# New costs, resources and ranks for the attention scheduler of a fused attention and mixture-of-experts kernel on one core

## The chip, the cores and the metric

The kernel runs on one core of a Trainium2 chip. The metric is the device time of one execution in microseconds, taken before the change from three runs; one more execution was profiled. TensorE is called PE here, VectorE DVE, ScalarE ACT, GpSimd POOL and SyncE SP.

## The reference

Three stages follow each other: windowed attention, a top-1 mixture of experts with a capacity, and a dense two-layer block with softplus. All is float32.

```python
# q, k, v: (2, 8, 768, 64); 8 global keys, a window of 96
scores = scale * q @ k.T + bias            # bias = -slope[h] * distance
scores = where(is_global | is_local, scores, -1e9)
a = softmax(scores);  x = (a @ v) -> (1536, 512)
# experts: E = 8, D = 512, F = 1024, capacity 384
e = argmax(x @ w_gate);  gate = max of softmax(x @ w_gate)
y = gate * (relu(x @ w1[e]) @ w2[e])       # rows over capacity give 0
# dense block: 512 -> 2048 -> 512
out = softplus(y @ w_in) @ w_out
```

## The kernel before, in words

The tokens are 12 tiles of 128 (2 batches of 6). Tiles 0 and 6 start a batch and have scores of 128 columns (short tiles); the others have 232, the window and the globals before it and the tile's own keys. The attention stage is followed by the expert stage (8 experts, their weights streamed from HBM) and the dense block; each of these begins when its input is there, and in the expert stage a step issues the loads of later weights itself.

For each tile i attention has these steps, which the code calls jobs. LD and LV load q, k and v by SP's queue (`load`, `load_v`). PQ and PK transpose q and k on PE (`prep`), Q and K copy them from PSUM (`keep`). S are the eight score matmuls (`scores`). B adds the bias and takes the maximum on DVE, one per head (`biased`); M1 writes one head's row of the long-tile bias table; E is the exponential on ACT with its sum (`expo`, sums in `den`). T transposes the probabilities of two heads on PE and C copies them (`transp`); V is P times V in two halves (`pv`); OT copies the result (`keep_o`). L, CH, G, R, SL choose the expert and the row's slot (`logits`, `choose`, `gate`, `ranks`, `slots`); X, N, SC transpose the rows back, weight them and scatter them to `xs_d` on POOL. DUP and VP copy the window's part of k and v for the next tile on POOL. ZF writes a block of zeros to `xs_d` (18 of them, by SP), CL and CV load and convert a piece of the dense block's weights (`conv_load`, `conv_step`; CV has one ACT and three DVE instructions), PU starts the load of expert 0's weights. At the end XR, FB and FA build the first expert's input on PE (`first_base`, `first_add`), and ST and CNT count.

The program of each engine is a fixed list, executed in order, each instruction waiting by semaphores for what it needs. This order is made when the kernel is built, by `arrange`: it takes again and again the job that can start first by its own times, and among equals the one of lowest rank (tile number plus `RANK`). A job has a cost per engine on which it may run, jobs it must follow, buffers it takes and gives back (`sizes`), a lag, and an earliest time `at`. Copies from PSUM may run on ACT or DVE; `LEAN` is a handicap for DVE there. The costs are used for the order alone; the chip knows nothing of them.

```python
key = (max(s, free[e] + SLACK) + (LEAN if e == "DVE" and len(x.cost) > 1 else 0.0), x.rank, s + c)
```

PSUM has eight banks: A (2) for preps, one part of the scores, logits, ranks and rows; B (3) for the other scores; C (2) for T; D (1) for P times V. In SBUF there are 8 score buffers `s_sb` (NS), 6 for transposed probabilities (NPT), 2 for q and k as loaded, 3 for v.

Of the kernel before, what the change touches and what calls it, by code (L numbers as in the profile page):

```python
# [96 lines left out]
class Job:  # L97

    def __init__(self, name, cost, run, after=(), take=(), give=(), rank=0.0, lag=0.1, at=0.0):
        self.name, self.cost, self.run, self.after, self.take, self.give = name, cost, run, after, take, give  # L100
        self.rank, self.lag, self.at = rank, lag, at


def arrange(jobs, sizes, free):
# [4 lines left out]
    while left:  # L109
# [33 lines left out]
SLACK, LEAN = 0, 0  # L143
RANK = {
# [223 lines left out]
def fast_path(ctx, tc, q, k, v, n_global, n_local, w_gate, w1, w2, cap, w_in, w_out, out, const):  # L368
# [87 lines left out]
    NS, NPT, NOT = 8, 6, 2  # L456
# [355 lines left out]
    def expo(n):  # L812
# [3 lines left out]
        if i not in dens:  # L816
            dens[i] = a2.tile([P, H], F32, name="den", bufs=3)
# [47 lines left out]
    def choose(i):  # L865
# [10 lines left out]
        ohb = a2.tile([P, E], BF16, name="ohb")  # L876
# [201 lines left out]
    either = lambda c: {"ACT": c, "DVE": c}  # L1078
    n_t = len(tiles)
    job(("TRI",), {"DVE": 0.5}, lambda e: start_tri(), [("M1", 0)])  # L1080
    for j in range(NSLOT // P):
        job(("ZF", j), {"SP": 0.1}, lambda e: zero_fill(1), at=10.0 + 1.9 * j)
    for i, (b, t) in enumerate(tiles):
        N, half = n_t - 1, 0.5 if t == 0 else 1.0
        prev = lambda *names: [(x, i - 2) for x in names] if i >= 2 else []
# [381 lines left out]
```

## Time and profile before

| what | value |
|---|---|
| median of 3 runs | 588.85 us (587.49 to 588.96) |
| the profiled execution | 588.03 us, span 586.1 us |
| mean granted clock of PE | 0.985 |
| PE busy | 557.9 us, 95% |
| DVE busy | 341.8 us, 58% |
| ACT busy | 275.9 us, 47% |
| POOL busy | 89.3 us, 15% |
| DMA | 91.86 MB, mean 157 GB/s |

The span is the time from the first to the last instruction; the rest of the profiled execution's time lies around it. The page's busy shares are means over stages with different limits, so the stages have to be read apart, by the table by stretches and by the timelines. A busy PE in the profile is not a PE at its peak, since ends of matmuls are modelled; start to start of neighbouring instructions is the safer measure.

### The profile page before, as it was taken

The page shows a single profiled execution, that of the slowest core. Times are in us where ns is not written, and L with a number is a line of the kernel's source. Part 1 is how long each engine was busy: PE and PEld are TensorE (multiplying, and loading weights), DVE is VectorE, ACT ScalarE, POOL GpSimd, SP SyncE. Part 2 cuts the span into 40 slices and gives each one's busy share as a digit, 9 for nine tenths or more (in the row PEclk, how much of TensorE's full clock was granted, in tenths as well). Part 3 has the DMA queues.
Part 4 walks back from the last instruction along what each step waited for, and adds up shares of the span by engine and source line. Part 5 has one row for each costly group of instructions (what it writes and reads, how often), then busy time and mean ns, then how long its engine had stood idle before and what let it go on. Part 6 is the DMA issues. An engine that isn't in the chain of part 4 may idle for free. (4 is left out here: it accounts for less than half of the span.)

```text
span 586.1 us, 9980 instructions
## 1 busy us (share of the span) xinstructions
PE 557.9 (95%) x3446; PEld 489.1 (83%) x3446; DVE 341.8 (58%) x998; ACT 275.9 (47%) x682; POOL 89.3 (15%) x123
## 2 busy tenths in 40 slices
PE   4889878989999999999999999999999999999995
PEld 3778756878999999999999888888888888888874
DVE  6677856874777873231575775654785363333451
ACT  3676946842664752322544454444554334323330
POOL 4101322110000000000354142100240020200201
PEclk9799979999999999999999999999999999999999
DMA  7996567825688779998844574432421200100101
GB/s 143 238 267 182 160 157 209 285 89 181 217 283 276 244 237 388 379 310 291 305 154 96 117 108 93 91 118 81 127 81 47 91 1 0 55 18 1 72 21 58
DMA packets 90832, 91.86 MB, mean 157 GB/s; under 512 B 43205, under 2 KB 61661, under 8 KB 90773
## 3 DMA queue, kind: packets, MB, share of 16 engines
q1 hardware_dynamic: 82709, 74.35, 43.7%
q10 hardware_dynamic: 5760, 10.49, 5.6%
q0 software_dynamic: 2304, 6.30, 2.9%
q8 instruction: 29, 0.48, 0.3%
q14 instruction: 30, 0.25, 0.1%
HBM read 71.71 MB, written 19.41 MB: 155 GB/s over the span
## 5 line engine op out<-in xcount | busy, mean ns | idle before, releaser
L1342 DVE SCALAR_TENSOR_TENSOR sa<-ps_m,sa 128x512 f32<-128x512 f32 x48 | 33.2, 692 | 106.9 <-ACT sa L1341 106.9
L1339 ACT ACTIVATE sa<-ps_m 128x512 f32<-128x512 f32 x48 | 28.7, 598 | 136.5 <-PE ps_m L1232 136.5
L1230 PE MATMUL ps_m<-zh,w1s 128*128 128x512 f32 x192 | 75.2, 392 | 0.0
L1231 PE MATMUL ps_m<-zl,w1s 128*128 128x512 f32 x192 | 74.8, 390 | 0.0
L1230 PE MATMUL ps_o<-w2s,g 128*128 128x512 f32 x192 | 74.8, 390 | 0.0
L1232 PE MATMUL ps_o<-w2s,g 128*128 128x512 f32 x192 | 74.8, 390 | 0.0
L1232 PE MATMUL ps_m<-zh,w1s 128*128 128x512 f32 x192 | 74.8, 389 | 0.0
L1231 PE MATMUL ps_o<-w2s,g 128*128 128x512 f32 x192 | 74.7, 389 | 0.0
L493 POOL TENSOR_TENSOR w1s<-raw,w1s 128x512 fp32r<-128x512 f32 x16 | 23.2, 1468 | 241.7 <-ACT w1s L505 241.6
L1281 PE MATMUL ps_y<-h,w 128*128 128x232 f32 (+4 forms) x320 | 59.1, 328 | 0.0
L1254 PE MATMUL ps_h<-xT,w 128*128 128x232 f32 (+4 forms) x320 | 58.7, 327 | 0.0
L819 ACT ACTIVATE s_sb<-s_sb,negm 128x232 f32<-128x232 f32 (+1 forms) x96 | 44.7, 468 | 25.4 <-DVE xg L923 19.2
L1254 PEld LDWEIGHTS ps_h<-xT,w 128*128 128x128 f32 x320 | 52.9, 190 | 0.7 <-ACT xT L1209 0.2
L1281 PEld LDWEIGHTS ps_y<-h,w 128*128 128x128 f32 x320 | 52.3, 190 | 0.5
L1230 PEld LDWEIGHTS ps_m<-zh,w1s 128*128 128x128 f32 x192 | 36.1, 188 | 8.3 <-DVE sa L1342 0.9
L1232 PEld LDWEIGHTS ps_o<-w2s,g 128*128 128x128 f32 x192 | 36.0, 188 | 7.9 <-DVE g L1350 0.4
L1230 PEld LDWEIGHTS ps_o<-w2s,g 128*128 128x128 f32 x192 | 36.0, 188 | 7.6 <-DVE g L1349 0.3
L1232 PEld LDWEIGHTS ps_m<-zh,w1s 128*128 128x128 f32 x192 | 36.0, 188 | 7.6
L1231 PEld LDWEIGHTS ps_o<-w2s,g 128*128 128x128 f32 x192 | 36.1, 188 | 7.5
L1231 PEld LDWEIGHTS ps_m<-zl,w1s 128*128 128x128 f32 x192 | 36.0, 188 | 7.5 <-DVE zl L1289 0.2
L1263 ACT ACTIVATE h<-ps_h 128x232 f32<-128x232 f32 (+4 forms) x40 | 13.3, 332 | 59.9 <-PE ps_h L1254 57.3
L86 DVE SCALAR_TENSOR_TENSOR ct<-csq,ct 128x256 int32<-128x256 int32 x64 | 33.2, 519 | 12.2 <-ACT csq L82 11.8
(208 smaller groups left out, 1133.6 us busy)
## 6 DMA issues: line engine op xcount, KB each, us to landing
w<-in_moe_w_dram SPq DMA_DIRECT2D x20, 1024.0 KB, 7.7
raw<-in_moe_w_dram SPq DMA_DIRECT2D x24, 512.0 KB, 5.3
cr<-in_moe_w_in_dram ACTq DMA_DIRECT2D x20, 256.0 KB, 3.3
cr<-in_moe_w_out_dram ACTq DMA_DIRECT2D x20, 256.0 KB, 3.9
xs_d<-early SPq DMA_DIRECT2D x18, 256.0 KB, 4.0
wi_d<-ct SPq DMA_DIRECT2D x32, 128.0 KB, 5.0
wo_d<-ct SPq DMA_DIRECT2D x32, 128.0 KB, 5.1
raw<-wi_d SPq DMA_DIRECT2D x8, 512.0 KB, 5.3
```

Of the source, the lines that this page charges most:

```text
L86: nc.vector.scalar_tensor_tensor(t, in0=u.bitcast(I32), scalar=3, in1=t, op0=ALU.logical_shift_left, op1=ALU.bitwise_or)
L493: eng.tensor_tensor(lo, raw, f32(hi), op=ALU.subtract)
L819: nc.scalar.activation(s_sb, s_sb, AF.Exp, bias=negm[:, n:n + 1], scale=-1.0, accum_out=dens[i][:, h:h + 1])
L1230: nc.tensor.matmul(ps, hi_l, hi_r, start=first, stop=False)
L1231: nc.tensor.matmul(ps, hi_l, lo_r, start=False, stop=False)
L1232: nc.tensor.matmul(ps, lo_l, hi_r, start=False, stop=last)
L1254: nc.tensor.matmul(ps, w[:, c, js], x[:, c, :], start=c == 0, stop=c == NC - 1)
L1263: nc.scalar.activation(h[:, :n], ps, AF.Relu)
L1281: nc.tensor.matmul(ys[ui, d], w[:, j, sl], h, start=f == 0, stop=f == NFE - 1)
L1339: nc.scalar.activation(a, ps, AF.Abs)
L1342: nc.vector.scalar_tensor_tensor(a, in0=ps, scalar=0.0, in1=a, op0=ALU.max, op1=ALU.add)
```

## The change

The change gives the scheduler other numbers and two new things. DMA transfers get costs as if SP's queue were an engine that moves the data (LD 2.9, LV 1.5, ZF 0.75, PU 5.0 instead of 0.1 to 0.3, with shorter lags), the zero fills may start from 21 us on instead of 10, and a job can also occupy a second engine (`also`: CV now takes 0.7 of ACT). Costs of single jobs are set anew, with copies at 0.47 (ACT) and 0.61 (DVE) of a unit instead of equal, LEAN is 0.3 instead of 0, and all 35 ranks are new. Ten score buffers instead of 8, eight for transposed probabilities instead of 6, six for `den` instead of 3, three for the one-hot rows instead of 2. The work itself is the same, instruction for instruction; order and engines change. All lines behind the first hunks move down by two or three, so L797 (scores) becomes L799, L737 and L739 (copies on ACT and DVE) become L739 and L741, and L1254 (the first expert matmul) L1257.

```diff
-    def __init__(self, name, cost, run, after=(), take=(), give=(), rank=0.0, lag=0.1, at=0.0):
+    def __init__(self, name, cost, run, after=(), take=(), give=(), rank=0.0, lag=0.1, at=0.0, also=()):
...
         free[e] = s + x.cost[e]
+        for o, c in x.also:
+            free[o] = max(free[o], s) + c
...
-SLACK, LEAN = 0, 0
+SLACK, LEAN = 0, 0.3
 RANK = {
-    "B": -2.6, "C": -1.84, "CH": 10.69, "CL": 12.72, "CNT": 9.95, "CV": -15.21, "DUP": 13.9, "E": -0.74, "FA":
+    "B": -12.52, "C": 9.58, "CH": -2.65, "CL": 10.16, "CNT": 7.36, "CV": 25.77, "DUP": 29.55, "E": 44.85,
...
-    NS, NPT, NOT = 8, 6, 2
+    NS, NPT, NOT = 10, 8, 2
...
-            dens[i] = a2.tile([P, H], F32, name="den", bufs=3)
+            dens[i] = a2.tile([P, H], F32, name="den", bufs=6)
...
-        ohb = a2.tile([P, E], BF16, name="ohb")
+        ohb = a2.tile([P, E], BF16, name="ohb", bufs=3)
...
-    either = lambda c: {"ACT": c, "DVE": c}
+    either = lambda c: {"ACT": 0.47 * c, "DVE": 0.61 * c}
...
-        job(("ZF", j), {"SP": 0.1}, lambda e: zero_fill(1), at=10.0 + 1.9 * j)
+        job(("ZF", j), {"SP": 0.75}, lambda e: zero_fill(1), at=21.0 + 1.7 * j)
...
-            job(("LD", i), {"SP": 0.2}, lambda e, i=i: load(i), prev("PQ", "PK") if i > 2 else [], lag=5.0)
+            job(("LD", i), {"SP": 2.9}, lambda e, i=i: load(i), prev("PQ", "PK") if i > 2 else [], lag=2.0)
...
-            job(("E", i, m), {"ACT": 0.5 if t else 0.42}, lambda e, n=n: expo(n), [("B", i, m)])
+            job(("E", i, m), {"ACT": 0.475 if t else 0.395}, lambda e, n=n: expo(n), [("B", i, m)])
...
-            job(("CV", i), {"DVE": 1.05}, lambda e: conv_step(1), [("B", i, H - 1)])
+            job(("CV", i), {"DVE": 1.02}, lambda e: conv_step(1), [("B", i, H - 1)], also=[("ACT", 0.7)])
...
-            job(("PU", i), {"SP": 0.3}, lambda e: pump(-1, 0), [("S", i)])
+            job(("PU", i), {"SP": 5.0}, lambda e: pump(-1, 0), [("S", i)])
```

What this does to the order is seen at three places. The first is PE's list from the scores of tile 0 (`qT_156`) to those of tile 1 (`qT_157`) and behind them. Before:

```order
L797 MATMUL ps_s<-kwin_130,qT_156 128x128 x8
L748 MATMUL ps_prep<-ident,kr 128x128 x4
L830 MATMUL ps_pt<-ident,s_sb 128x128 x2
L748 MATMUL ps_prep<-ident,qr 128x128 x4
L748 MATMUL ps_prep<-ident,kr 128x128 x4
L748 MATMUL ps_prep<-ident,qr 128x128 x4
L830 MATMUL ps_pt<-ident,s_sb 128x128 x2
L849 MATMUL ps_pv<-pT,vt_125 64x128 x4
L797 MATMUL ps_s<-kwin_131,qT_157 128x232 x8
```

And now:

```order
L799 MATMUL ps_s<-kwin_130,qT_156 128x128 x8
L750 MATMUL ps_prep<-ident,kr 128x128 x4
L750 MATMUL ps_prep<-ident,qr 128x128 x4
L832 MATMUL ps_pt<-ident,s_sb 128x128 x4
L799 MATMUL ps_s<-kwin_131,qT_157 128x232 x8
L832 MATMUL ps_pt<-ident,s_sb 128x128 x4
L851 MATMUL ps_pv<-pT,vt_125 64x128 x8
L750 MATMUL ps_prep<-ident,kr 128x128 x4
L865 MATMUL ps_lg<-wg,oT 128x16 x4
L750 MATMUL ps_prep<-ident,qr 128x128 x4
L832 MATMUL ps_pt<-ident,s_sb 128x128 x4
```

Of the four q/k transposes that stood ahead of tile 1's scores two are left, tile 1's own; tile 2's and its P times V stand behind them. In the list before, another eight instructions of T, prep and P times V follow before tile 2's scores.

The second place is ACT's list around tile 9 to 10, from one O copy (`oT`) on. Before:

```order
L819 ACTIVATE s_sb,den<-s_sb,negm 128x232 x5
L885 ACTIVATE lg,gs<-lg,nmx 128x8
L737 COPY pT<-ps_pt 128x512 x3
L819 ACTIVATE s_sb,den<-s_sb,negm 128x232
L737 COPY kwin_131<-ps_prep 128x4x128
L819 ACTIVATE s_sb,den<-s_sb,negm 128x232
L737 COPY pT<-ps_pt 128x512
L557 DMA cr<-in_moe_w_in_dram 128x512
L82 ACTIVATE csq<-cr 128x256
L737 COPY qT_156<-ps_prep 128x512
```

And now:

```order
L739 COPY oT<-ps_pv 128x512
L739 COPY pT<-ps_pt 128x512
L739 COPY qT_156<-ps_prep 128x512
L739 COPY pT<-ps_pt 128x512
L821 ACTIVATE s_sb,den<-s_sb,negm 128x232 x2
L739 COPY pT<-ps_pt 128x512 x2
L739 COPY kwin_131<-ps_prep 128x4x128
L887 ACTIVATE lg,gs<-lg,nmx 128x8
L559 DMA cr<-in_moe_w_in_dram 128x512
L82 ACTIVATE csq<-cr 128x256
L821 ACTIVATE s_sb,den<-s_sb,negm 128x232 x6
```

Now all four copies of transposed probabilities, that of q and that of k of a tile are ACT's, ahead of the exponentials of the next tile's later heads. Over the whole stage ACT has 80 of the 82 copies, where it had 62; DVE keeps 2 of 20.

The third place is SP's queue behind the first loads, from tile 2's loads on (`vt_127` is tile 2's v, `early` is the block of zeros). Before:

```order
L624 DMA qr<-in_q_dram 128x8x64
L614 DMA kr<-in_k_dram 96x8x64
L615 DMA kr<-in_k_dram 32x8x64
L614 DMA vt_127<-in_v_dram 96x8x64
L615 DMA vt_127<-in_v_dram 32x8x64
L1037 DMA xs_d<-early 128x512
L624 DMA qr<-in_q_dram 128x8x64
L614 DMA kr<-in_k_dram 96x8x64
L615 DMA kr<-in_k_dram 32x8x64
L1037 DMA xs_d<-early 128x512
```

And now:

```order
L626 DMA qr<-in_q_dram 128x8x64
L616 DMA kr<-in_k_dram 96x8x64
L617 DMA kr<-in_k_dram 32x8x64
L626 DMA qr<-in_q_dram 128x8x64
L616 DMA kr<-in_k_dram 96x8x64
L617 DMA kr<-in_k_dram 32x8x64
L616 DMA vt_125<-in_v_dram 96x8x64
L617 DMA vt_125<-in_v_dram 32x8x64
L626 DMA qr<-in_q_dram 128x8x64
L616 DMA kr<-in_k_dram 96x8x64
L617 DMA kr<-in_k_dram 32x8x64
L1039 DMA xs_d<-early 128x512 x3
```

Tile 2's v (`vt_127`) now stands just ahead of these rows, before its q and k, and the first zero fills come behind the load of tile 4, three at a time; tile 3's q and k follow tile 2's at once. From there on the fills stand in groups of one to three between the loads up to that of tile 9: 17 of them, and three v loads, lie between the load of tile 4 and that of tile 8.

## Rows read from the trace of the kernel before

**Rows 1.** Table by stretches, whole core: us, busy time of each engine, clock, DMA share, GB/s.
```profile
30.00:40.00 10.00, 9.66 (x100) 8.26 (x99) 8.18 (x49) 5.85 (x20) 1.12 (x2) 1.00 1.07 244
...
80.00:90.00 10.00, 9.35 (x64) 7.47 (x64) 5.48 (x27) 4.92 (x17) 1.03 (x3) 0.66 0.33 93
...
200.00:300.00 100.00, 99.92 (x719) 98.78 (x718) 43.95 (x100) 37.13 (x95) 8.72 (x6) 1.00 0.88 303
```

**Rows 2.** PE's timeline, 10 to 145 us: start, us, line, tiles, shape, [idle before <- releaser].
```profile
16.22 1.09 PE L748 MATMUL ps_prep<-ident,kr 128*128 128x128 f32 x4 [4.40 <-DMA kr<-in_k_dram]
...
20.43 2.61 PE L797 MATMUL ps_s<-kwin,qT 64*128 64x232 f32 x16
...
53.43 1.84 PE L797 MATMUL ps_s<-kwin,qT 64*128 64x232 f32 x16
...
83.65 3.42 PE L797 MATMUL ps_s<-kwin,qT 64*128 64x232 f32 x16
...
113.14 1.84 PE L797 MATMUL ps_s<-kwin,qT 64*128 64x232 f32 x16
...
130.32 0.18 PE L889 MATMUL ps_rk<-ohb,tri 128*128 128x8 bf16 x1 [0.59 <-DVE nmx L879]
...
134.65 1.83 PE L1023 MATMUL ps_x<-here,xg 128*128 128x232 f32 x8 [1.03 <-DVE xg L923]
...
136.34 4.97 PE L1254 MATMUL ps_h<-xT,w 128*128 128x232 f32 x24
```

**Rows 3.** Waits of PE, 0 to 130 us: total, times, longest.
```profile
PE ps_pt L830 <- ACT pT L737: 4.0, 2, 2.0
...
PE ps_pv L849 <- ACT pT L737: 3.2, 3, 1.7
```

**Rows 4.** PE's timeline, stretches without a gap, and the short tile's scores.
```profile
47.95 1.07 PE L830 MATMUL ps_pt<-ident,s_sb 128*128 128x128 f32 x8
...
48.86 0.60 PE L748 MATMUL ps_prep<-ident,kr 128*128 128x128 f32 x4
...
49.82 0.44 PE L849 MATMUL ps_pv<-pT,vp 104*64 104x128 f32 x4
...
50.85 1.09 PE L830 MATMUL ps_pt<-ident,s_sb 128*128 128x128 f32 x8
...
55.20 1.06 PE L863 MATMUL ps_lg<-wg,oT 128*128 128x16 f32 x8
...
56.58 1.04 PE L830 MATMUL ps_pt<-ident,s_sb 128*128 128x128 f32 x8
...
64.08 1.16 PE L797 MATMUL ps_s<-kwin,qT 64*128 64x128 f32 x16
```

**Rows 5.** VectorE's timeline, 9 to 23 us.
```profile
9.54 0.32 DVE L726 SCALAR_TENSOR_TENSOR dtmp<-rel,nlval,dtmp 128x104 f32<-128x104 f32 x1
...
11.03 0.47 DVE L731 TENSOR_SCALAR bias<-early 128x232 f32<-128x232 f32 x2
...
14.34 0.22 DVE L721 TENSOR_SCALAR early<-early 128x128 f32<-128x128 f32 x1
...
14.81 0.46 DVE L731 TENSOR_SCALAR bias<-early 128x232 f32<-128x232 f32 x2
...
22.73 0.40 DVE L807 CUSTOM_DVE_ANT_0 s_sb<-ps_s,bias 128x232 f32<-128x232 f32 x1
```

**Rows 6.** ScalarE's timeline, 39 to 43 us.
```profile
39.33 0.47 ACT L819 ACTIVATE s_sb<-s_sb,negm 128x232 f32<-128x232 f32 x1
...
41.03 1.04 ACT L737 COPY pT<-ps_pt 128x512 f32<-128x512 f32 x2
```

**Rows 7.** DMA issues by line: count, KB each, median us to landing.
```profile
xs_d<-early SPq DMA_DIRECT2D x18, 256.0 KB, 4.0
...
qr<-in_q_dram SPq DMA_DIRECT2D x11, 256.0 KB, 4.5
...
kr<-in_k_dram SPq DMA_DIRECT2D x11, 192.0 KB, 4.5
```

More of the change, by code (lines that the diff above doesn't have):

```diff
@@ L97 @@
 class Job:
-    def __init__(self, name, cost, run, after=(), take=(), give=(), rank=0.0, lag=0.1, at=0.0):
+    def __init__(self, name, cost, run, after=(), take=(), give=(), rank=0.0, lag=0.1, at=0.0, also=()):
         self.name, self.cost, self.run, self.after, self.take, self.give = name, cost, run, after, take, give
-        self.rank, self.lag, self.at = rank, lag, at
+        self.rank, self.lag, self.at, self.also = rank, lag, at, also
 def arrange(jobs, sizes, free):
@@ L1095, in fast_path @@
             for step, (p, c) in enumerate((("PQ", "Q"), ("PK", "K"))):
-                job((p, i), {"PE": 0.44}, lambda e, i=i, s=step: prep(i, s), [("LD", i)] if i >= 2 else [],
+                job((p, i), {"PE": 0.44 * (2.0 if i <= 2 else 1.0)}, lambda e, i=i, s=step: prep(i, s), [("LD", i)] if i >= 2 else [],
                     take=[("A", (p, i), 0.0)], lag=0.25, at=9.5 if i == 1 else 0.0)
-                job((c, i), either(0.59), lambda e, i=i, s=step: keep(e, i, s),
+                job((c, i), either(1.0), lambda e, i=i, s=step: keep(e, i, s),
                     [(p, i)] + prev("S") + (prev("DUP") if step else []), give=[("A", (p, i), 0.0)])
@@ L1101, in fast_path @@
             ([("K", i)] if i else []) + ([("S", i - 1)] if i else []), at=8.0)
-        job(("S", i), {"PE": 2.0 if t else 1.3}, lambda e, i=i: scores(i),
+        job(("S", i), {"PE": 1.97 if t else (1.2 if i else 2.1)}, lambda e, i=i: scores(i),
             ([("Q", i), ("K", i)] if i else []) + ([("DUP", i - 1)] if t else []),
@@ L1126, in fast_path @@
                 take=[("D", i, 0.0)] * (g == 0), give=[("pT", i * 4 + 2 * g + x, 0.0) for x in range(2)], lag=0.25, at=11.0)
-        job(("OT", i), either(0.59), lambda e, i=i: keep_o(e, i), [("V", i, 1)], take=[("oT", i, 0.0)],
+        job(("OT", i), either(1.0), lambda e, i=i: keep_o(e, i), [("V", i, 1)], take=[("oT", i, 0.0)],
             give=[("D", i, 0.0)])
-        job(("RS", i), {"DVE": 0.34}, lambda e, i=i: over_den(i), [("E", i, H - 1)])
+        job(("RS", i), {"DVE": 0.33}, lambda e, i=i: over_den(i), [("E", i, H - 1)])
         job(("L", i), {"PE": 0.9}, lambda e, i=i: logits(i), [("OT", i)], take=[("A", ("L", i), 0.0)], lag=0.25)
-        job(("CH", i), {"DVE": 1.5}, lambda e, i=i: choose(i), [("L", i), ("RS", i)],
-            give=[("A", ("L", i), 1.25)])
+        job(("CH", i), {"DVE": 1.43}, lambda e, i=i: choose(i), [("L", i), ("RS", i)],
+            give=[("A", ("L", i), 1.15)])
         job(("G", i), {"ACT": 0.3}, lambda e, i=i: gate(i), [("CH", i)], lag=0.2)
@@ L1135, in fast_path @@
             take=[("A", ("R", i), 0.0)], lag=0.25)
-        job(("SL", i), {"DVE": 1.0 + (0.5 if i >= n_t - 2 else 0.0)}, lambda e, i=i: slots(i),
+        job(("SL", i), {"DVE": 0.85 + (0.45 if i >= n_t - 2 else 0.0)}, lambda e, i=i: slots(i),
             [("R", i), ("G", i)] + ([(("SC", i - 5), 3.0, True)] if i >= 5 else []), give=[("A", ("R", i), 0.7)])
         job(("X", i), {"PE": 0.44}, lambda e, i=i: rows(i), [("OT", i), ("R", i)], take=[("A", ("X", i), 0.0)], lag=0.25)
-        job(("N", i), {"DVE": 0.68}, lambda e, i=i: weighted(i), [("X", i), ("SL", i)],
+        job(("N", i), {"DVE": 0.62}, lambda e, i=i: weighted(i), [("X", i), ("SL", i)],
             give=[("A", ("X", i), 0.0), ("oT", i, 0.0)])
@@ L1156, in fast_path @@
     sizes = {"A": 2, "B": 3, "C": 2, "D": 1, "s": NS, "pT": NPT, "oT": NOT}
-    for _, e, x in arrange(jobs, sizes, {"PE": 7.2, "DVE": 7.6, "ACT": 8.0, "POOL": 8.0, "SP": 6.0}):
+    for _, e, x in arrange(jobs, sizes, {"PE": 7.2, "DVE": 7.6, "ACT": 8.0, "POOL": 8.0, "SP": 11.5}):
         x.run(e)
```

25 lines of the change are left out of this document (13 added, 12 removed), and 8 rows, old and new, of the table RANK.

## The prediction

> **What bounds the kernel now.** I read the table by stretches first. From 200 to 300 us the tensor engine (PE) is busy 99.92 of 100 us at full clock [rows 1]: the expert stage has nothing to give, and its length follows its start. In the attention stage PE stands idle or slow: at 80 to 90 us its mean granted clock is 0.66. Second view, PE's timeline [rows 2], by the score matmuls S(i) of tile i (L797): S1 starts at 20.43, S5 at 53.43, S11 at 113.14, and the first expert matmul (L1254) at 136.34. So the time is 136.34 us of attention and then 449.8 us that begin when attention ends. Third, what full speed is, from a stretch without a gap [rows 4], start to start: two transposes of probabilities (T) 0.91, so 0.455 each; two q/k transposes (PQ, PK) 0.96, so 0.48 each; one half of P times V 1.03; logits and rows back (L and X) 1.38 together, X about 0.47 of it; a score step 1.77 (53.43 to 55.20), of a short tile 1.16 less the overlap, 1.09. A long tile is then 1.77 + 4 x 0.455 + 0.96 + 2.06 + 1.38 = 8.0 us of PE, the short one (tile 6) some 5.6. From S5 to S11 the kernel before takes 59.7 us for six tiles, 9.95 each. The rest is waiting, for loads (4.40 us before the k transposes at 16.22 [rows 2]) and for ScalarE's copies (4.0 and 3.2 us [rows 3]), and low clock after some of it: S8 at 83.65 takes 3.42 us for the 16 instructions that take 1.84 at S11 [rows 2].
>
> **The change, part by part.** No instruction is added or removed: order, the engine of 18 copies, and buffers change. I sum the new start of the expert stage in three pieces.
>
> *To S5.* In the new order S1 stands ahead of tile 2's q/k transposes, so it no longer stands behind the load that ended at 16.22. The bound becomes VectorE and then ScalarE. VectorE: two of tile 0's eight pairs (bias row, bias add) are over at 9.54, where the long-tile table begins [rows 5]. A pair is 14.34 to 14.81, 0.47 us. The change does the other six first: 9.54 + 2.8 = 12.4; the table's head (9.54 to 11.03) 1.5 and its first row 0.24: 14.1. To the second bias add of tile 1 there are 0.5 of waiting for the last exponential of tile 0, four short instructions at 0.22 (an estimate from the bias rows), two table rows 0.46 and two bias adds at 0.32 (0.40 busy less 0.08 of overlap [rows 5]): 16.6. From there ScalarE has ten steps in its queue up to the copy of tile 3's k: five exponentials, O of tile 0, k and q of tile 2, one T copy, k of tile 3, each some 0.47 (an exponential 0.47; two copies 1.04 with 0.1 of overlap [rows 6]): 21.4. S2 with its handover: 21.8. Then the rows of PE's order are longer than either other engine's: S2 to S3 is S, 2 T, X, V half, 4.2; S3 to S4 S, two preps, V half, 2 T, L, 5.6; S4 to S5 S, 5 T, 3 V halves, L and X, 3 preps, 10.0. S5: 21.8 + 19.8 = 41.6.
> What is late next here is a transfer. Tile 3's load now stands behind vt of tile 2 and the load of tile 2, and lands at about 16.2 + 1.0 + 2.1 = 19.3 (256 and 512 KB at 244 GB/s [rows 1, 7]). PE wants it at 19.5: tile 2's k, landed at 17.2, then a prep, L and another prep and a T, 2.3. And the zero fills now stand in groups of 1 to 3 between the loads of tiles 4 to 9. From the load of tile 4 to that of tile 8, about 19 to 47 us, 17 fills, five q/k loads (0.52 MB each), three v loads and three weight pieces (0.26 each) are 8.7 MB, which at the 244 GB/s of a stretch with DMA share 1.07 [rows 1] is 35.5 us in 28. Bounds: nothing (each load has some 8 us from its issue to its use) and 7.5. I take 1.5, near the lower end, because by 6.5 MB up to it the load of tile 7 is through at 19.3 + 26.9 = 46.2 and wanted at 41.6 + 6.0 = 47.6, so that only what follows it is late. **S5: 43.1.**
> The Trainium skill, "DMA: Bandwidth & Descriptors", section "Where 436 GB/s comes from", puts transfers from HBM to SBUF at some 358 GB/s; by that the 8.7 MB would be an estimated 24 us in the 28, and the term of 1.5 nothing. The row's 244 GB/s at a full DMA share speaks against it here.
>
> *S5 to S11.* In the new order every T belongs to the tile before the scores that PE has just done; ten score buffers (8 before) allow that. So no T waits for a fresh exponential. Counted from the order: S 5 x 1.77 + 1.09 = 9.9; 20 T and 4 short ones at half 10.0; 10 V halves and 2 short ones at half 11.3; six L and X 8.3; 11 preps 5.3; ranks 0.4. Sum 45.2. ScalarE has, with 80 of 82 copies on it (62 before), 8 x 0.47 + 7 x 0.47 and about 0.7 of small ones per long tile, 7.8 us, 0.2 below PE's 8.0; VectorE loses 18 copies. For the handovers that don't fit I take 0.6 per tile, the size of the small wait at 130.32 [rows 2], so 3.6; bounds 0 and 1.0 (rival 2). **S11: 43.1 + 45.2 + 3.6 = 91.9**, against 113.14.
>
> *S11 to the expert stage.* 23.2 us before, for the same instructions. The base matmuls (L1015), which now cover part of the wait for the last choice at 130.32, move behind the last rows back, so that wait grows; the 1.03 at 134.65 should go, since the base then stands between the last rank and the last addition. Bounds -1.6 and +1.5, I take +0.4: 23.6. **Expert stage: 115.5**, 20.8 us earlier.
>
> *Other edits.* More den and one-hot buffers: nothing, they only free waits. Scatters: four in a row after tile 6, behind the last zero fill; POOL has room (tile 0's would hold only the sixth weighted sum, five buffers). The 18 fewer copies on VectorE cost ScalarE what is counted above. Expert 0's weights are issued after S9 and S10, which is still some 30 us before their use; the rest of the weights moves with the stage.
>
> Sum: the profiled execution has 588.03 us with a span of 586.1; 588.03 - 20.8 = **567 us**. The median of the runs, 588.85, is 0.8 above it, which is inside what a measurement can tell (about 0.3%, 1.8 us).
>
> **Rivals.**
> 1. *Loads bind.* The fills between the loads make the q/k of tiles 5 to 8 late by the full 7.5, and PE's waits bring the lower clock for one stretch like 80 to 90 (10 us at 0.66, 3.4 lost [rows 1]): 567 - 1.5 + 7.5 + 3.4 = 576. For it: the 1.07 share. Against: the slack of 8 us per load.
> 2. *ScalarE binds.* It is at 7.8 of 8.0. If PE's waits for its copies stay as they are (4.0 + 3.2 = 7.2 us [rows 3]) and grow with the copies, by 80 over 62, they are 9.3 us, 1.0 in each of nine tiles, instead of 3.6: 573. Against: T now has a whole tile of lead, and the copy that PE waits for at once stands early in ScalarE's order.
> 3. *The clock.* Short waits of PE, of which the new order has several per tile, let the granted clock fall to the lower of its two levels (1.2 of 2.4 GHz) for part of the time. If S5 to S11 ran at a mean of 0.83, half way to the 0.66 of [rows 1], 48.8 us become 58.8: 577. Against: the mean granted clock of the span is 0.985 in the table above, though PE waits in every tile. The Trainium skill, "TensorE: Matmul & The Clock Gate", section on the second failure mode, says that small idle gaps between groups of matmuls, from cycling through PSUM banks, made the clock swing between its levels; no row here ties the fall to short gaps.
> 4. *Slower: the load loop.* q/k tiles have two buffers: the load of tile n+2 waits for PQ of n, and from PK of n+2 to PQ of n+2 lie a prep, two V halves, S, X and T, 5.2 us. Two tiles cannot be shorter than a load's landing plus 5.2. With the landings of [rows 7] (4.5 median) that is under 10 of 16 us. It decides once a load takes 15.1 us: then a tile is 10.15, and 21.8 + 9 x 10.15 = 113.1 is the old S11. At 16 us in a queue full of fills a tile is 10.6, S11 117.2, and the end 592. For it: one queue issues all, in order, and its v loads and stores wait ahead of q/k loads. Against: no row near 15 us.
> 5. *Given back.* Attention ends earlier, but PE then waits for weights in the expert stage, whose DMA share is 0.88 [rows 1]: 588. Against: those loads are issued by the stage's own steps.
>
> **How the numbers follow.** Forecast 0.62; loads 0.12; ScalarE 0.09; clock 0.06; loop 0.07; given back 0.04. Faster by over 0.3% are the first four, 0.89; of rival 5 most is within 0.3%, 0.03; slower 0.08. Low end: without the allowances, 41.6 + 45.2 + 23.2 - 1.6 gives 108.4, 560 us. High end: the dearest of the faster rivals, 577, and 2 us for two of them in part: 579. Outside lie rivals 4 and 5 and some of the edges, under 2 in 10.
>
> **What would show it.** S1 near 12.5, S2 near 22, S5 at 42 to 44, S11 at 88 to 95, the first L1257 (L1254 before) at 112 to 118; PE's clock at 1.00 from 30 us on; no wait of PE for a load over 2 us; ScalarE over 9 tenths between S4 and S11; expert stage 449 to 451 us long. Wrong: waits for kr or qr of 3 us and more between 25 and 60 us (rival 1, or 4 if the loads take 15), PE waiting for pT copies over 1 us in every tile (2), a clock under 0.9 in most stretches (3), or an expert stage over 452 (5).

## The result, and the profile after

The changed kernel takes 580.26 us (median of 4 runs, 577.89 to 581.63) against 588.8 us (4 runs, 587.49 to 588.96): a ratio of 0.9856, with a 95% interval of 0.9816 to 0.9896. It is faster by 8.5 us, where 21 were forecast, and lies 1.3 us above the range's upper end. The profiled execution took 579.16 us, with a span of 577.3 (588.03 and 586.1 before).

The table gives the starts of PE's steps, in us, in the profiled executions; the last columns are kernels of the experiments below. S(i) are tile i's scores, and the last row but one the first matmul of the expert stage.

| step | before | forecast | after | e_both | e_tight_sw | e_pu |
|---|---|---|---|---|---|---|
| S1 | 20.43 | 12.5 | 12.44 | 12.43 | 12.49 | 12.14 |
| S2 | 26.13 | 21.8 | 27.04 | 24.38 | 22.58 | 22.21 |
| S5 | 53.43 | 43.1 | 47.27 | 44.60 | 42.80 | 42.44 |
| S8 | 83.65 | | 70.01 | 67.05 | 64.96 | 64.60 |
| S9 | 94.47 | | 85.24 | 75.07 | 72.98 | 72.67 |
| S11 | 113.14 | 91.9 | 102.26 | 90.81 | 88.72 | 88.41 |
| expert stage | 136.34 | 115.5 | 127.34 | 122.27 | 123.03 | 118.92 |
| median of the runs | 588.8 | 567 | 580.26 | 574.0 | 574.2 | 572.81 |

From its first matmul to the end of the span the expert stage and what follows take 577.3 - 127.34 = 450.0 us, and 449.8 before: nothing is lost or gained there. All of the story lies between 12 and 127 us. Of the 13.3 us between the forecast and the median, 11.8 arise there; the profiled execution is 1.1 us faster than the median, and the rest is rounding. PE's timeline of the changed kernel, the rows that answer to [rows 2]:

```profile
12.44 1.84 PE L799 MATMUL ps_s<-kwin,qT 64*128 64x232 f32 x16
...
19.70 1.09 PE L750 MATMUL ps_prep<-ident,kr 128*128 128x128 f32 x4 [3.67 <-DMA kr<-in_k_dram]
...
27.04 1.84 PE L799 MATMUL ps_s<-kwin,qT 64*128 64x232 f32 x16
...
47.27 1.84 PE L799 MATMUL ps_s<-kwin,qT 64*128 64x232 f32 x16
...
53.91 0.63 PE L750 MATMUL ps_prep<-ident,kr 128*128 128x128 f32 x4 [0.46 <-DMA kr<-in_k_dram]
...
76.16 0.60 PE L750 MATMUL ps_prep<-ident,kr 128*128 128x128 f32 x4
...
83.34 0.69 PE L851 MATMUL ps_pv<-pT,vp 104*64 104x128 f32 x4 [6.58 <-POOL vp L647]
...
85.24 2.92 PE L799 MATMUL ps_s<-kwin,qT 64*128 64x232 f32 x16
...
102.26 1.84 PE L799 MATMUL ps_s<-kwin,qT 64*128 64x232 f32 x16
...
119.69 0.18 PE L891 MATMUL ps_rk<-ohb,tri 128*128 128x8 bf16 x1 [1.55 <-DVE nmx L881]
...
127.34 4.97 PE L1257 MATMUL ps_h<-xT,w 128*128 128x232 f32 x24
```

Three rows are idle for more than 1 us: 3.67 at 19.70, for the k of tile 2; 6.58 at 83.34, for a copy on POOL; 1.55 at 119.69, for the last choice. Between 27.04 and 76.16 the longest wait is the 0.46 at 53.91. The table by stretches, with the columns of [rows 1]:

```profile
20.00:27.10 7.10, 6.78 (x38) 6.51 (x36) 2.33 (x12) 4.52 (x13) 0.50 (x1) 0.58 0.85 175
...
30.00:40.00 10.00, 10.00 (x106) 8.53 (x108) 8.54 (x51) 9.80 (x37) 1.06 (x2) 1.00 0.90 247
...
40.00:50.00 10.00, 10.00 (x117) 8.83 (x114) 7.54 (x41) 10.00 (x33) 1.36 (x4) 1.00 0.85 241
...
83.30:88.10 4.80, 4.76 (x33) 3.91 (x33) 0.73 (x4) 0.85 (x4) 2.05 (x3) 0.57 0.82 195
...
119.70:127.40 7.70, 7.53 (x40) 6.86 (x40) 5.28 (x29) 0.94 (x3) 1.94 (x2) 0.78 0.18 72
```

From 30 to 50 us PE is busy all the time at full clock, and ScalarE is busy 9.80 and 10.00 of 10. Behind each of the three waits the granted clock is low: 0.58 for 7.1 us, 0.57 for 4.8, 0.78 for 7.7 (the first two mostly, the third partly at the lower of its two levels, 1.2 of 2.4 GHz). By these rows, if the work scales with the clock, the stretches would have been 3.0, 2.1 and 1.7 us shorter at full clock (an estimate). The waits of PE from 10 to 130 us name who was waited for; these are the largest and the smallest:

```profile
PE ps_pv L851 <- POOL vp L647: 6.6, 1, 6.6
...
PE ps_lg L865 <- ACT oT L739: 0.2, 1, 0.2
```

The waits for ScalarE's copies of [rows 3], 7.2 us before, are gone; all that is left of waits for ScalarE is 0.2. What took the place of part of them is POOL.

**Who held tile 2's k.** SP's queue, start of each issue and its length:

```profile
12.58 0.58 SPq L616 DMA_DIRECT2D kr<-in_k_dram  x1
...
17.74 0.31 SPq L617 DMA_DIRECT2D kr<-in_k_dram  x1
...
18.14 0.40 SPq L626 DMA_DIRECT2D qr<-in_q_dram  x1
```

k is loaded in two pieces. The first is issued at 12.58, the second (L617) not before 17.74, and everything behind it on SP waits as well. SP's waits up to 90 us say for what:

```profile
SPq L617 <- DMA cr<-in_moe_w_in_dram: 9.6, 2, 5.0
...
SPq L626 <- DMA cr<-in_moe_w_in_dram: 4.3, 1, 4.3
```

`cr` is a piece of the dense block's weights, and it is loaded by ScalarE's queue:

```profile
13.13 0.38 ACTq L559 DMA_DIRECT2D cr<-in_moe_w_in_dram  x1
```

The list of waits in the built program has the link. These are SP's rows for tile 2's q and k and for tile 3's q, and ScalarE's load:

```
SP   L626 DMA qr<-in_q_dram 128x8x64 [waits DMAHW5_49,PE_49]
SP   L616 DMA kr<-in_k_dram 96x8x64 [waits DMAHW7_49,DMAHW6_49,PE_49]
SP   L617 DMA kr<-in_k_dram 32x8x64 [waits DMAHW7_49]
SP   L626 DMA qr<-in_q_dram 128x8x64 [waits DMAHW0_49,PE_49]
ACT  L559 DMA cr<-in_moe_w_in_dram 128x512 [waits DMAHW7_49]
```

The program has eight semaphores for the transfers of SP's and ScalarE's queues and hands them out in turn. A transfer that gets one again is issued only when the transfer that had it before has landed. In the changed kernel the first weights' piece stands early in ScalarE's list and got number 7, and the next to get it was the second piece of tile 2's k. The piece issued at 13.13 landed shortly before 17.74, and SP stood until then. In the kernel before, that piece was issued at 25.42.

**Who held tile 7's v.** POOL's timeline (L933 scatters, L778 copies the window's k, L646 and L647 that of v):

```profile
62.84 1.15 POOL L933 DMA_INDIRECT xs_d<-xg,sl  x1 [6.94 <-DMA ids_d<-zi]
...
69.42 0.98 POOL L933 DMA_INDIRECT xs_d<-xg,sl  x1 [5.42 <-DVE negm L809]
...
75.21 0.97 POOL L933 DMA_INDIRECT xs_d<-xg,sl  x1 [4.81 <-DVE negm L809]
...
78.67 0.97 POOL L933 DMA_INDIRECT xs_d<-xg,sl  x1 [2.50 <-DVE ct L84]
...
81.45 1.17 POOL L646 COPY vp<-vt 8x512 f32<-8x512 f32 x2 [1.29 <-issue]
...
82.68 0.61 POOL L647 COPY vp<-vt 96x512 f32<-96x512 f32 x1
```

A scatter takes POOL 1 us, but the next starts 6.6, 5.8 and 3.5 us later. The list of waits shows why: the second to fourth scatter each wait for the semaphore of the one before (DMASW0, 1, 2), that is until its rows have landed, since all write the same tensor; the first waits for the zero fills; and tile 7's v copy (L646) has a wait for the fourth (DMASW3), though it touches none of the scatter's tiles. So four in a row held POOL from 62.84 to 81.45, and P times V of tile 7, which PE had reached at 76.76, began at 83.34. SP stood in the shadow of the same wait: it issued nothing between 69.9 and 83.3, because the next load of v wanted that copy done.

### The profile page after: what moved, and what is told of

It reads as the page before. It is cut to its first block, busy times and chain, and to the rows that moved or that the text cites. A ratio compares the mean times of both kernels' runs of the same rounds, so it can differ in the third digit from the quotient of the medians.

```text
span 577.3 us, 9953 instructions
## 1 busy us (share of the span) xinstructions
PE 552.8 (96%) x3446; PEld 489.0 (85%) x3446; DVE 332.5 (58%) x980; ACT 283.8 (49%) x700; POOL 89.3 (15%) x123
## 5 line engine op out<-in xcount | busy, mean ns | idle before, releaser
L1257 PE MATMUL ps_h<-xT,w 128*128 128x232 f32 (+4 forms) x320 | 58.8, 328 | 0.0
L1257 PEld LDWEIGHTS ps_h<-xT,w 128*128 128x128 f32 x320 | 52.9, 190 | 0.6 <-ACT xT L1212 0.2
L1266 ACT ACTIVATE h<-ps_h 128x232 f32<-128x232 f32 (+4 forms) x40 | 13.3, 331 | 60.0 <-PE ps_h L1257 57.4
L1353 DVE TENSOR_TENSOR g<-sa,g 128x512 fp32r<-128x512 f32 x48 | 39.1, 814 | 1.7
```

The source lines that it names most:

```text
L1257: nc.tensor.matmul(ps, w[:, c, js], x[:, c, :], start=c == 0, stop=c == NC - 1)
L1266: nc.scalar.activation(h[:, :n], ps, AF.Relu)
L1353: nc.vector.tensor_tensor(gl_, a, f32(gh), op=ALU.subtract)
```

## The experiments

All variants of the changed kernel but a_buf keep the order that its scheduler makes and move single jobs in it by hand, so that nothing else changes places; b_s1 does so with the kernel before:

```diff
-    for _, e, x in arrange(jobs, sizes, {"PE": 7.2, "DVE": 7.6, "ACT": 8.0, "POOL": 8.0, "SP": 11.5}):
-        x.run(e)
+    plan = [(e, x) for _, e, x in arrange(jobs, sizes, {"PE": 7.2, "DVE": 7.6, "ACT": 8.0, "POOL": 8.0, "SP": 11.5})]
+    for name, behind in (
+            (("SC", 1), ("VP", 7)),
...
+    ):
+        j = next(r for r in plan if r[1].name == name)
+        plan.remove(j)
+        plan.insert(1 + next(n for n, r in enumerate(plan) if r[1].name == behind), j)
+    for e, x in plan:
+        x.run(e)
```

The diffs below show the pairs (job, the job that it goes behind); from e_vp to e_pu_zf each kernel has the moves of the one above it, unless its diff takes them out. The eight semaphores are handed out anew along each new order. Totals of neighbouring variants lie within each other's intervals, and those of e_pool and e_cl overlap the changed kernel's; the steps in the profiles tell them apart. Each kernel has one profile, and a step can differ by over 1 us between kernels whose lists are the same up to it (S2 is at 24.38 in e_both and at 25.75 in e_vp), so a difference of 1 us in one step shows nothing.

### The two stalls, singly and together

e_pool, the scatters spread out:

```diff
+            (("SC", 1), ("VP", 7)), (("SC", 2), ("VP", 8)), (("SC", 3), ("VP", 9)),
+            (("SC", 4), ("SC", 3)), (("SC", 5), ("VP", 10)), (("SC", 6), ("SC", 5)),
```

> The changed kernel with six scatters moved back in POOL's list: the first stays, the second goes behind the window copies of v for tile 7, the third behind those of tile 8, the others behind those of tiles 9 and 10. Theory P (each scatter holds POOL until the one before it has landed, 3 to 6.5 us, and four of them in a row kept tile 7's v from PE): PE's wait of 6.6 us at 76.8 falls under 1 us, the granted clock of the stretch behind it (0.57 for 4.8 us) goes back to 1.00, some 2 us more; 580.3 - 8.6 = 571.7 us. Theory F (the zero fills are late, so the first scatter and all that is behind it are late whatever stands in between): tile 7's v copy still starts after 79 us, gain under 2 us, 579. Theory L (loads bind: SP issues nothing from 69.5 to 83.3, which was only the shadow of the same wait): PE waits instead for q, k or v of tiles 9 to 11, gain under 4 us, 576 or more.

Measured: 577.32 us (ratio to before 0.9806, 0.9763 to 0.985). The wait at tile 7 is gone, S9 starts at 78.55 (85.24) and S11 at 94.28 (102.26), 8.0 us earlier at that point, close to the 8.6 of theory P, and neither F nor L. PE's clock is 1.00 from 70 to 100 us. But the expert stage starts only 2.1 us earlier, at 125.27, and the total misses theory P's 571.7 by 5.6. POOL's timeline near the end:

```profile
102.11 0.97 POOL L933 DMA_INDIRECT xs_d<-xg,sl  x1 [4.25 <-DVE ga L904]
...
105.56 0.97 POOL L933 DMA_INDIRECT xs_d<-xg,sl  x1 [2.48 <-DMA xs_d<-xg,sl]
...
109.02 0.97 POOL L933 DMA_INDIRECT xs_d<-xg,sl  x1 [2.48 <-DMA xs_d<-xg,sl]
...
109.98 0.63 POOL L647 COPY vp<-vt 96x512 f32<-96x512 f32 x1
```

My own list now had three scatters in a row ahead of tile 11's v copy (L647, 109.98), and PE waited 4.6 us for it. The stall moved from tile 7 to tile 11.

e_cl, the weights' load moved:

```diff
+            (("CL", 1), ("LD", 3)),
```

> The changed kernel with one job moved: the first load of a piece of the dense block's weights (issued by ACT, 13.13 us) goes behind tile 3's loads. Theory S (the load's semaphore is the one that SP's list wants for the second piece of tile 2's k, so SP stands from 13.2 to 17.7 until that load has landed): tile 2's k lands 4 us earlier, PE's wait of 3.67 at 16 goes, and so does the low clock behind it; tile 2's scores from 27.0 to 22 to 23.5, total 580.3 - 4.5 = 575.8. Theory B (transfers: tile 2's v now goes ahead of its q and k and the queue is full): k still lands at 19 or later, tile 2's scores within 1 us of 27, total 580. Third possibility, given back: tile 2's scores come 4 us earlier, but tile 7 then waits 4 us longer for POOL, total 579 to 580.

Measured: 576.65 us (0.9816, 0.9764 to 0.9868). S2 starts at 23.37, in the range of theory S; the expert stage at 123.18, 4.2 us earlier. The wait for POOL at tile 7 is 6.5 us as before (the zero fills and scatters came earlier with the rest), so nothing was given back there. B and the third possibility fall. The size is less sure than the mechanism: with the same move S2 is at 24.38 in e_both and 25.75 in e_vp, a gain of 1.3 to 3.7 us. By S11 (100.18 for 102.26) the lead is 2.1 us, after two waits of 0.72 and 1.05. The other half of the 4.2 comes behind the last choice: the 40 matmuls from there to the expert stage, 7.70 us at a clock of 0.78 in the changed kernel, take 5.60 at 1.00 here, behind the same wait of 1.55:

```profile
117.60:123.20 5.60, 5.59 (x40) 5.30 (x40) 4.48 (x26) 0.94 (x3) 1.68 (x2) 1.00 0.12 48
```

e_swap, tile 2's v behind its q and k:

```diff
+            (("LV", 2), ("LD", 2)),
```

> The changed kernel with only tile 2's v load moved behind its q and k loads, as the kernel before has it; the weights' piece stays where it is and still lands at 17.7. Theory S: the held instruction is then the second piece of v, tile 2's k lands by 16.5, tile 2's scores at 22 to 23.5, total about 576; tile 3's loads are still issued at 18 and PE may wait up to 1 us for them. Theory B by contention with the weights' piece: k as late as before, total 580. That the order of v against q and k is itself the cause (0.26 MB, 1 us): a gain of 1 us, 579.

Measured: 579.88 us (0.9855, 0.9812 to 0.9898), no gain. PE's timeline:

```profile
17.79 0.63 PE L750 MATMUL ps_prep<-ident,kr 128*128 128x128 f32 x4 [1.19 <-DMA kr<-in_k_dram]
...
24.10 1.09 PE L750 MATMUL ps_prep<-ident,kr 128*128 128x128 f32 x4 [3.36 <-DMA kr<-in_k_dram]
```

Tile 2's k does come earlier (wait 1.19). The held instruction is now the second piece of v, which SP issues at 17.91, and behind it tile 3's loads start at 18.32; PE's list wants tile 3's k ahead of S2 and waits 3.36 us for it. So the held queue costs the same whichever load stands at its head: S2 at 27.56. Theory S is right in the mechanism and my price of 1 us for tile 3 was wrong.

e_both, the moves of e_pool and e_cl:

> Both moves together. If the two are the whole of what the prediction missed up to tile 11's scores: 580.3 - 8.6 - 4.5 = 567.2 us, the first matmul of the expert stage at 114 to 116. If they are not independent (the stall of POOL is fed by the same zero fills that SP issued late): between 567 and 571. If loads bind in a faster attention stage, or ScalarE does: over 571, with the new waits of PE naming which.

Measured: 574.0 us (0.9764, 0.9716 to 0.9813), S11 at 90.81. That is 1.1 us from the forecast 91.9, in part by luck: S2 is still 2.6 us later than the 21.8, and the work from S2 to S11 takes 66.4 us where 70.1 were forecast. What remains is behind S11: 31.5 us to the expert stage instead of 23.6, with a wait of 5.1 us for tile 11's v copy on POOL. The total is that of the last branch, over 571, but what binds behind S11 is neither loads nor ScalarE.

### What binds then

e_vp takes that copy out from behind the scatters:

```diff
+            (("VP", 11), ("V", 9, 1)), (("SC", 7), ("VP", 11)),
```

> The kernel with both moves, and the window copy of v for tile 11 moved ahead of the eighth to tenth scatters on POOL (there it stood behind three of them and PE waited 5.1 us for it, with a low clock from 100 to 120). Theory P: that wait goes and tile 11's scores stay at 90.8. How much of it comes through depends on the chain of scatters itself: each waits until the one before it has landed, the tenth is issued at 109.5, the rows are read back from 112 to 115, and the base matmuls (L1017) cannot start before. If that chain is now the bound: PE waits 3 to 4 us at L1017 instead, first expert matmul at 120.5, 572 us. If it is not: 90.8 + 23.2 = 114.0, 565.5 us. If POOL's list was not the cause: no change, 574.

Measured: 575.42 us (0.9776, 0.974 to 0.9813). S11 at 91.86, no wait for POOL, and yet the expert stage starts at 123.29. PE's timeline, the waits behind S11:

```profile
109.29 0.18 PE L891 MATMUL ps_rk<-ohb,tri 128*128 128x8 bf16 x1 [1.55 <-DVE nmx L881]
...
115.25 3.98 PE L1017 MATMUL ps_x<-ident,xr 128*128 128x128 f32 x16 [5.26 <-DMA xr<-xs_d]
```

The base matmuls (L1017) wait 5.26 us for rows that are read back when the tenth scatter has landed, and the clock of 110 to 120 falls to 0.54. The tenth scatter starts at 109.55, where e_both has 109.49, so taking the copy out from behind the scatters did not bring it forward. The chain of scatters has become the bound, as the first branch said, at 123.3 instead of 120.5.

e_spq loads the weights' pieces by SP's queue in the attention stage:

```diff
-    conv_q = [nc.scalar]
+    conv_q = [nc.sync]
...
+    conv_q[0] = nc.scalar
     routed = moe_x["routed"]
```

> As the run before, but the pieces of the dense block's weights are loaded by SP's queue in the attention stage, not by ACT's, so that no load of SP waits for a semaphore that a transfer of another queue holds. Theory S: SP's time in such waits (18 us in the kernel with both moves) falls under 4, tile 2's scores at 23.4 or earlier, the last zero fill is issued at 50 or earlier (54.7), the first scatter at 56 or earlier (60.0), the chain of scatters ends earlier by as much, total 569 or less. Rival: the transfers themselves bind (a DMA share of 0.9 from 20 to 60): fills and first scatter within 1.5 us of before, total as in the run before within 1.5.

Measured: 573.33 us (0.9748, 0.9698 to 0.9797). In the list of waits the eight semaphores now go round in SP's own order, and SP waits for no weights' load any more, as theory S said. But that lets the chain start only a little earlier: against e_both the last fill is issued 1.4 us earlier (at 53.35), the first scatter 2.2 (57.84), the tenth 1.0 (108.53); against e_vp, the kernel above it, 2.7, 3.1 and 1.0. These are neither branch's numbers. That the transfers hold part of what the semaphores held (DMA share 0.89 to 1.00 from 20 to 60 us) is a reading, not shown. The wait at L1017 is 5.37.

e_tight puts the scatters closer together, e_tight_sw also lets PE start earlier:

```diff
-            (("SC", 3), ("VP", 9)), (("SC", 4), ("SC", 3)), (("SC", 5), ("VP", 10)), (("SC", 6), ("SC", 5)),
+            (("SC", 3), ("SC", 2)), (("SC", 4), ("VP", 9)), (("SC", 5), ("SC", 4)), (("SC", 6), ("VP", 10)),
...
+            (("LV", 2), ("LD", 3)),
```

The last line is e_tight_sw's alone.

> As the kernel with SP loading the weights' pieces, with the scatters on POOL closer together: the fourth right behind the third, the fifth and sixth behind tile 9's window copy, the seventh behind tile 10's. Theory C (the chain of scatters is the bound, and from the third to the seventh my own list spaced it 8 us where a landing takes 5.5): the tenth scatter at 105 to 106 (108.5), PE's wait at L1017 2 to 3 us (5.4), first expert matmul at 118 (121.5), 569.8 us. Rival: with the expert's weights in flight from 80 to 95 us a landing takes as long as the transfers ahead of it whenever it is issued; the tenth within 1 us of 108.5, 573.

> As the run before, and tile 2's v is loaded behind tile 3's q and k instead of ahead of tile 2's. If the chain of scatters binds, a lead of PE at the start is worth nothing: tile 2's scores 1 us earlier (22.9 for 24.0), the first expert matmul within 1 us of the run before, total the same. If PE's own list binds: 1 us and the low clock behind it, 1.5 to 2 us faster.

Measured: 573.87 (0.9766, 0.9723 to 0.981) and 574.2 us (0.9771, 0.9729 to 0.9813). In e_tight the tenth scatter stands at 109.14: the rival holds, my spacing was not the limit. e_tight_sw says it most plainly: PE is 2.2 us ahead at S2 and at S11 (88.72 for 90.93), and the expert stage starts no earlier (123.03 for 122.64). Its wait, 5.58 in e_tight, grows by the 2.2 gained and by the 0.9 by which the tenth scatter is later:

```profile
115.75 3.89 PE L1017 MATMUL ps_x<-ident,xr 128*128 128x128 f32 x16 [8.67 <-DMA xr<-xs_d]
```

The fourth to seventh and the tenth scatter of e_tight_sw on POOL:

```profile
76.29 0.97 POOL L933 DMA_INDIRECT xs_d<-xg,sl  x1 [6.61 <-DVE den L860]
...
84.79 0.98 POOL L933 DMA_INDIRECT xs_d<-xg,sl  x1 [6.47 <-DVE den L860]
...
92.08 0.97 POOL L933 DMA_INDIRECT xs_d<-xg,sl  x1 [6.30 <-DMA vt<-in_v_dram]
...
97.79 0.98 POOL L933 DMA_INDIRECT xs_d<-xg,sl  x1 [4.11 <-DVE st L1053]
...
110.06 0.98 POOL L933 DMA_INDIRECT xs_d<-xg,sl  x1 [2.47 <-DMA xs_d<-xg,sl]
```

The fourth to seventh are 5.7 to 8.5 us apart, while the weights of expert 0, issued from 72.7 and 81.3 us on, are in flight. e_pu moves those loads behind the last load of v, to 84.8 us and later:

```diff
+            (("PU", 9), ("LV", 11)), (("PU", 10), ("PU", 9)),
```

> As the run before (tile 2's v behind tile 3's q and k), with the loads of expert 0's weights (four of 1 MB) moved from behind tile 10's and 11's loads of q and k to behind the last v load, so from about 82 and 89 us to 92. Theory D (from the fourth scatter on each landing takes 7 to 8.5 us because the weights fill the queues): the fourth to seventh scatter 5 to 6 us apart, the tenth at 104 to 107 (110.1), the wait at L1017 3 to 6 us (8.7), first expert matmul at 118 to 120 (123.0), 570 us. Rival: the same bytes only delay the seventh to tenth, the tenth at 109 or later, 574, or the expert stage waits for its weights.

Measured: 572.81 us (0.9741, 0.9712 to 0.977), the lowest median of all variants. It is 7.4 us below the changed kernel by the medians, 6.8 by the ratios, and the intervals of the two ratios don't touch; that of e_tight_sw overlaps it. The same scatters in e_pu, and the table by stretches:

```profile
72.95 0.98 POOL L933 DMA_INDIRECT xs_d<-xg,sl  x1 [3.88 <-DVE ct L86]
...
76.74 0.98 POOL L933 DMA_INDIRECT xs_d<-xg,sl  x1 [0.50 <-DVE den L860]
...
82.17 0.97 POOL L933 DMA_INDIRECT xs_d<-xg,sl  x1 [4.45 <-PE ps_s L799]
...
85.62 0.98 POOL L933 DMA_INDIRECT xs_d<-xg,sl  x1 [1.41 <-PE ps_pt L832]
...
106.04 0.97 POOL L933 DMA_INDIRECT xs_d<-xg,sl  x1 [4.01 <-DVE nmx L881]
```

```profile
16.00:22.30 6.30, 4.55 (x38) 4.08 (x38) 5.53 (x31) 5.79 (x20) 0.51 (x1) 1.00 1.10 202
...
30.00:40.00 10.00, 10.00 (x107) 8.95 (x103) 8.35 (x45) 10.00 (x35) 1.50 (x3) 1.00 1.07 315
...
80.00:90.00 10.00, 10.00 (x114) 8.83 (x110) 8.95 (x49) 10.00 (x37) 2.56 (x3) 1.00 0.59 176
...
90.00:100.00 10.00, 10.00 (x110) 8.63 (x106) 7.89 (x49) 9.53 (x31) 1.59 (x2) 1.00 1.04 386
```

They are 3.5 to 5.4 us apart, with a DMA share of 0.59 from 80 to 90 us, and for the spacing theory D holds: the tenth at 106.04, the wait at L1017 4.33, the expert stage at 118.92. The weights come at 90 to 100 us instead, at 386 GB/s, and there the scatters stretch again (94.20 to 101.05).

e_pu_zf pulls five zero fills forward:

```diff
+            (("ZF", 13), ("ZF", 12)), (("ZF", 14), ("ZF", 13)), (("ZF", 15), ("ZF", 14)),
+            (("ZF", 16), ("LD", 7)), (("ZF", 17), ("ZF", 16)),
```

> As e_pu, and five zero fills moved ahead: three from behind tile 7's loads to ahead of them, two from behind tile 6's v and tile 8's loads to behind tile 7's. Theory C (the chain of scatters begins with the last zero fill and PE has slack against it): the first scatter at 52 to 53 (56.7), tile 7's k up to 3 us late for PE, the chain earlier by 2 to 4 us, first expert matmul 116 to 118, 567 us. Rival: what the loads lose PE loses, and the tenth scatter waits for tile 9's rows: as e_pu within 1.

Measured: 574.42 us (0.9768, 0.9738 to 0.9799): neither the forecast nor the rival. The last fills are issued at 46.97 (51.14), yet the first scatter starts at 55.29 (56.21). The fills are not what held it: from issue to landing they take 5.3 us at most (5.2), so all have landed by 52.7. What held the scatter for the rest is not shown. The second scatter stands behind tile 7's v copy in POOL's list and starts at 63.36 (62.72), so an earlier first one would have gained nothing. PE waits 0.58 for a k at 49.44, and S11 is 1.0 later. The fourth to seventh scatter are 3.5 to 5.2 us apart as in e_pu, but the tenth is at 108.09 and the expert stage at 122.21. So the closer spacing is seen in two kernels, and the earlier expert stage in one of them only.

### Parts of the change

a_buf keeps the changed kernel's scheduler and takes the score and transposed buffers back:

```diff
-    NS, NPT, NOT = 10, 8, 2
+    NS, NPT, NOT = 8, 6, 2
```

> The changed kernel with 8 score buffers and 6 for transposed probabilities instead of 10 and 8; the order is made anew from these. Theory (from the prediction: ten buffers let every transpose belong to the tile before): PE waits again for ScalarE's exponentials and copies, 4 us or more between tile 2's and tile 11's scores, and the steps between scores become irregular; 585 us. Rival: buffers do nothing, the gain is in ranks and costs: 580 within 1.5.

Measured: 585.8 us (0.9962, 0.9935 to 0.9989), 5.5 slower than the changed kernel, near the number that theory gave, but only in part by its mechanism. From S2 to S7 it takes 35.2 us (36.2 with the buffers). PE's waits for ScalarE are 2.7 us in all (0.2), of which 1.6 lie between S2 and S11, where the theory asked 4 or more. The largest wait is again for POOL:

```profile
78.17 3.47 PE L799 MATMUL ps_s<-kwin,qT 64*128 64x232 f32 x16 [7.74 <-POOL kwin L778]
```

The order made anew again has four scatters in a row on POOL, this time with the window's k copy behind them. But that wait is only 1.2 us longer than the changed kernel's 6.58. With 2.5 more for ScalarE and 0.8 for loads the waits come to 4.5 of the 6.0 us by which the expert stage starts later (133.31); the rest is not taken apart here. So this run does not show what ten buffers are worth; it shows that such an order comes out of the scheduler under other settings too.

b_s1 makes one move by hand in the kernel before:

```diff
+            (("PK", 2), ("S", 1)), (("PQ", 2), ("PK", 2)), (("K", 2), ("PQ", 2)), (("Q", 2), ("K", 2)),
```

> The kernel before, with one edit by hand: tile 2's q and k transposes and their copies go behind tile 1's scores. Theory: tile 1's scores no longer stand behind the load that ends at 16.22, they start at 14 to 15 (20.43), tile 2's at 22 to 23 (26.13), the rest of the order is unchanged and keeps the lead; 588.8 - 3.5 = 585.3. Rival, given back: ScalarE's list or the next load makes up for it, tile 5's scores within 1 us of 53.4, 588.8.

Measured: 589.53 us (1.0014, 0.9995 to 1.0032). The rival holds. PE's timeline:

```profile
15.01 3.12 PE L797 MATMUL ps_s<-kwin,qT 64*128 64x232 f32 x16
...
23.91 0.63 PE L748 MATMUL ps_prep<-ident,kr 128*128 128x128 f32 x4 [2.43 <-DMA kr<-in_k_dram]
...
26.09 1.84 PE L797 MATMUL ps_s<-kwin,qT 64*128 64x232 f32 x16
```

S1 is 5.4 us earlier and S2 at 26.09 where it was (26.13): in that list tile 4's k transposes stand ahead of S2, and their load, issued 1.4 us later than before (19.55 for 18.19), ends the next wait. Getting S1 out from behind a load is worth nothing alone here.

## Why the prediction was wrong, step by step

- **S1 at 12.5**: right, 12.44.
- **S2 at 21.8**: wrong by 5.2. The failed sentence is "tile 2's k, landed at 17.2": it reckoned bytes at a rate and took SP's issues to follow each other. SP was held from 13.2 to 17.7 by a semaphore that a transfer of ScalarE's queue had (e_cl: S2 at 23.37; e_pu, with the other orders of loads too: 22.21). The wait of 3.67 and the low clock behind it, 3.0, are 6.7, so by this account the engines' part of the step was 1.4 us too dear.
- **S2 to S5**: 20.2 for 19.8 + 1.5. Of the 1.5 allowed for loads 0.4 was used, and the row's 244 GB/s was no ceiling: at the same DMA share of 1.07, e_pu moved 315 GB/s from 30 to 40 us, and 386 with the 1 MB loads from 90 to 100. The Trainium skill, "DMA: Bandwidth & Descriptors", section "Where 436 GB/s comes from", has some 358 GB/s for transfers between HBM and SBUF, by which the term was nothing. The 315 lies below that figure, the 386, which counts all traffic of the stretch, above it, and the measurement decides.
- **S5 to S11**: 55.0 for 48.8. The failed step is in "Other edits": "four in a row after tile 6 [...] POOL has room". It gave the scatters no price on the path, without a reason but POOL's room; a scatter does take POOL only 1 us. What decides is its landing, 3.5 to 6.6 us from one issue to the next here, with tile 7's v queued behind four of them: 6.58 of waiting and 2.1 of low clock, 8.7. Without them the step is 46.3; in e_both it is 46.2. The work, 45.2, was right, and the handovers were 1.0 where 3.6 were allowed: ScalarE at 10 of 10 with 80 copies cost PE next to nothing.
- **S11 to the expert stage**: 25.1 for 23.6. The wait for the last choice grew from 0.59 to 1.55, as the step said. It had no term for the low clock behind that wait, 1.7 us (0.78 over 7.7 us). In e_cl, with the same wait and the clock at 1.00, the step took 23.0. Why the clock fell behind this wait in one execution and not in the other the runs don't show.
- **Expert stage**: as said, 450.0 us.
- **The sum**: 5.2 - 1.1 + 6.2 + 1.5 = 11.8 us too early at the expert stage. The two stalls with the clock behind them are 15.4 and the tail 1.5; the rest of the working was 5.0 too dear (1.4 + 1.1 + 2.5), so the error in the sum is smaller than the two steps that failed.
- **The rivals**: rivals 1 and 3, 576 and 577, come nearest to the measured time, but their marks aren't there (for rival 1, no wait for q or k over 0.46 us from 27 us on). ScalarE (2), the load loop (4) and the expert stage (5) did not bind. The clock (3) did not fall in the regular tiles, 27 to 76 us, where PE has only short waits; it fell behind the stalls. Missing were a rival on POOL's queue and one on SP being held by a transfer of another queue. Even with both stalls cured 567 would not have been reached in this form: the chain of scatters, up to the rows read back at L1017, then binds at 119 to 123 us (e_vp to e_pu). How far an order with fewer transfers beside the scatters could go below 119 stays open.

## What to carry to other kernels

An instruction that starts a transfer is short on its engine, but if the next one waits for its landing, a row of them is a chain: price each by issue to landing, and look at what is queued behind the last. When a scheduler is given transfer times, ask which resources are still not in its model; here they were the semaphores that two queues share and the order among writes to one tensor. And before crediting a step that starts earlier, find the next load that its successor needs: a lead is worth what the last arrival at the join lets through.

## What the runs showed of the hardware

- A scatter of 128 rows of 2 KB landed in 2.7 us at best and 7.4 at most in the changed kernel. Scatters that wait for each other followed at 3.46 us with a DMA share of 0.2 (e_vp, 100 to 110 us), at 6.6 and 5.8 us in the changed kernel from 62.8 to 75.2 us with small loads in the queues (share 0.89 from 60 to 70), and at up to 8.5 us while 1 MB loads ran (e_tight_sw). The Trainium skill, "DMA: Bandwidth & Descriptors", section "Anatomy of one DMA", fits 2.0 us plus the bytes at 436 GB/s, an estimate of 2.6 us for these 256 KB; the quiet queue agrees, the full one doesn't, and the measured spacing decides.
- What a wait costs behind it: the clock was 1.00 from 16 to 22.3 us of e_pu, with a wait of 1.10 in it, but 0.58 and 0.57 behind the waits of 3.67 and 6.58 of the changed kernel and 0.54 around the one of 5.26 in e_vp. Waits between these went either way: behind 1.55 us the clock was 0.78 in the changed kernel and 1.00 in e_cl. The two stalls of the changed kernel cost an estimated 3.0 and 2.1 us once more that way.
